# Gated mix of windowed decode attention and an MLP on one core: inputs transposed on VectorE, rest rows on 64 partitions, one exponential and one transpose per group, paired sums, a masked query product

## The chip, the core and the metric

The kernel runs on one core of a Trainium2 chip. A core has five engines, each with its own instruction stream: TensorE (PE in the profile, with its weight loads as PEld), VectorE (DVE), ScalarE (ACT), GpSimd (POOL) and SyncE (SP). SP and ACT issue loads from HBM; 16 DMA engines carry them out. Data is worked on in SBUF (128 partitions), and TensorE writes its products to PSUM (8 banks of 512 fp32 for each partition). Engines wait for each other and for loads by semaphores.

The metric is the device time of one execution in microseconds (us). The kernel before takes 368.27 us, the median of three runs (368.18 to 368.58).

## The reference

One decode step for 8 batch rows: attention over the last 2048 positions of a key and value cache (16 heads of keys and values, 32 query heads, so two query heads share one), and an MLP with a layer norm in front; a sigmoid gate mixes the two.

```python
B, D, Hq, Hkv, Sk, Dh, F = 8, 576, 32, 16, 8192, 128, 4608
W = 2048                                     # window: the last 2048 positions
g = sigmoid((x * gate_w).sum(-1, keepdims=True))
# a: attention
q = (x @ wq).reshape(B, 1, Hq, Dh)
k, v = k_cache[:, :, Sk - W:], v_cache[:, :, Sk - W:]   # each head of k, v serves two of q
p = softmax(einsum("bhqd,bhkd->bhqk", q, k) * Dh ** -0.5)
a = einsum("bhqk,bhkd->bhqd", p, v).reshape(B, 1, Hq * Dh) @ wo
# b: MLP
y = (x - mean(x)) / sqrt(var(x) + 1e-5)
b = gelu(y @ w1 + b1) @ w2 + b2
return g * a + (1 - g) * b                   # bf16 throughout; x is (8, 1, 576)
```

The inputs that matter for size are the two windows, 8 x 16 x 2048 x 128 bf16 each (67 MB each), wq and wo (4.7 MB each), w1 and w2 (5.3 MB each).

## The kernel before

**How it is planned.** The kernel is not written engine by engine. It adds operations, each with an engine, the operations it depends on and an estimated cost, to a plan (`_Plan`, L39). `schedule` (L62) runs a list schedule on those estimates and so fixes each engine's order; it then strikes out waits that others imply. `emit` (L176) writes the instructions of an engine in that order, with all waits of an operation ahead of its first instruction. On the chip each engine runs its list strictly in order; an operation whose input is late holds all that stands behind it.

**Slots.** Nine slots of 2 MB in SBUF (`NSLOT`, `take_slot` L679) take all big loads. SP issues the loads in the order of `stream` (L641 to L656): wq and w1 first (L450 to L454), then K units, from the sixth on in turn with V units, a block of wo after every eighth V unit, b2 and at last four pieces of w2 (the last one cut in four). A unit is half of one head's cache: four batch rows of that head, 128 partitions of 16 KB. A load waits until its slot has been read: K by the transposes on DVE (L748), V by the products with P (L795).

**Start.** ACT issues x, the gate vector (two loads) and b1 (L444 to L447). PE transposes x (`tr_in`, L482), b1 (`b1_fn`, L495) and the normalised y; DVE copies them from PSUM (L504, L509). DVE computes the gate's dot product, mean and variance on 8 partitions (L462 to L480). wq has 576 rows: 512 lie as four rows on each of 128 partitions, and the rest of 64 rows is cut in halves of columns, 128 half rows (L450); the stationary operand is padded with zeros in two forms (`xz`, L458) to fit. w1 is laid out the same way (L454). The query (`q_fn`, L541) and the MLP's first layer (`h`, L575) are made by four concurrent 32-column tiles of PE. The query is selected and spread to `q4` (L562 to L571). Slots 0 to 2 hold wq and slots 3 to 5 hold w1 until these products are done.

**A group** is two heads of K, four units (32 query rows: two heads, eight batch rows, two query heads each). For each half unit DVE transposes K in 32x32 blocks (L748) into one of two buffers, and PE multiplies with a block-diagonal query, two weight loads and eight matmuls of 512 columns (L754 to L761, helpers L395 and L410); the group's first product starts with a mask (L757). POOL fills the block-diagonal query with four copies (L737 to L742). After the fourth unit come, on DVE, the maximum over 2048 columns (L689) and ten small operations that combine it across partitions; on ACT four exponentials of 512 columns with their sums (L703); on DVE four transposes of P (L708) and the sums (L711, L712). `sums` (L715) adds across partitions on PE, takes reciprocals and scales by the gate (L724), once for each of the eight groups.

**V** (`v_batch`, L784): 64 matmuls on four tiles for each group of four units, a selection by three predicated copies (L811, L812), a fold on PE (L820), a copy on ACT (L826) and a scaling on POOL for each of two heads (L835). In the last group each unit is a batch of its own (`FULL`, L674). After every second group, eight query heads feed a product with a block of wo (L839 to L859).

**End.** All products with wo and w2, and b2, add up in one PSUM bank that `acc0` (L616) has cleared; DVE and ACT copy it out in halves (L891), and ACT stores it (L899).

## Time and profile before

| | |
|---|---|
| median of three runs | 368.27 us |
| the profiled execution | 368.25 us |
| its span, first to last instruction | 366.5 us |
| TensorE clock granted, mean | 0.81 |
| read from HBM | 154.31 MB |
| instructions | 2945 |

The span is the time from the first to the last instruction in the profile; the 1.75 us between span and time of the execution lie before and after. In the page's slices each digit is the busy share of a fortieth of the span (9.16 us) in tenths. Windows list, for each stretch, the busy time and count of PE, PEld, DVE, ACT and POOL, then PE's granted clock, the mean busy share of the 16 DMA engines and the GB/s that they moved. A row of the timeline has start, length, engine, line, operation, output and input, count and, in brackets, the idle time before it with what ended it. `DMA` rows in the chain of waits run from issue to landing; SPq and ACTq are rows in which SP or ACT issue a load. q1 is the queue of SP's loads, q10 of ACT's, q8 and q14 those of instructions.

### The profile page before, as it was taken

The numbers are of one execution on the slowest core, as the hardware profiler recorded it, in microseconds if no ns is written. First come the engines' busy times: TensorE is split into PE (matmuls) and PEld (weight loads), VectorE is DVE, ScalarE is ACT, GpSimd is POOL, SyncE is SP. The second block draws the span as 40 slices with busy tenths as digits, with TensorE's granted clock in tenths as the row PEclk, the third lists the DMA queues.
The fourth block names the chain that finished last, engine by engine and source line by source line (L and its number), as shares of the span: only waits on it lengthen the run. The fifth ranks groups of instructions, "written<-read, shape, count | busy, mean of one in ns | idle before, by whom it ended". The sixth has DMA issues, their size and how long they took to land.

```text
span 366.5 us, 2945 instructions
## 1 busy us (share of the span) xinstructions
PE 228.7 (62%) x1397; PEld 46.3 (13%) x935; DVE 227.1 (62%) x307; ACT 29.3 (8%) x84; POOL 25.6 (7%) x72
## 2 busy tenths in 40 slices
PE   0256972891974388762973298654975297666576
PEld 0211000100110012100210012000200022013233
DVE  0824999788585666549854665469654874566210
ACT  1010003003000110003000200003000300002000
POOL 8010001001010101001010101010000101001000
PEclk9986897997798869666996879686986679698558
DMA  8999999999999999999999999999999999999994
GB/s 342 429 405 427 429 435 434 433 436 429 427 429 431 428 432 435 431 431 428 429 430 428 424 439 431 429 433 431 427 431 429 435 430 431 431 429 425 424 429 196
DMA packets 11463, 154.52 MB, mean 422 GB/s; under 512 B 1300, under 2 KB 1588, under 8 KB 2104
## 3 DMA queue, kind: packets, MB, share of 16 engines
q1 hardware_dynamic: 11392, 154.29, 98.6%
q8 instruction: 9, 0.15, 0.1%
q10 hardware_dynamic: 56, 0.04, 0.1%
q14 instruction: 6, 0.05, 0.0%
HBM read 154.31 MB, written 0.01 MB: 421 GB/s over the span
## 4 chain that ended last, share of the span: by engine, by line
DMA 48%; DVE 23%; PE 20%; issue 3%; ACT 3%; SPq 2%
DMA arena<-in_A_k_cache_dram 33%; DVE arena L748 13%; PE ps L395 12%; DMA arena<-in_A_v_cache_dram 9%; DMA arena<-in_B_w_dram 6%; PE ps L410 5%; DVE arena L689 4%; PE ps L795 4%; ACT arena L703 3%; DVE arena L708 2%; DVE arena L698 1%; DVE arena L692 1%; SPq L776 1%; SPq L878 0%; SPq L453 0%
## 5 line engine op out<-in xcount | busy, mean ns | idle before, releaser
L748 DVE STREAM_TRANSPOSE arena<-arena 128x2048 f32<-128x2048 f32 x64 | 145.0, 2294 | 53.8 <-DMA arena<-in_A_k_cache_dram 48.2
L395 PE MATMUL ps<-arena 128*128 128x512 bf16 x402 | 138.4, 456 | 5.9 <-DVE arena L748 3.3
L410 PE MATMUL ps<-arena 128*128 128x512 bf16 x124 | 58.7, 473 | 80.9 <-ACT arena L703 40.7
L795 PE MATMUL ps<-arena 128*32 128x512 bf16 x512 | 36.9, 437 | 13.9 <-DMA arena<-in_A_v_cache_dram 13.9
L410 PEld LDWEIGHTS ps<-arena 128*128 128x128 bf16 x136 | 15.2, 112 | 210.6 <-DVE arena L748 90.0
L703 ACT ACTIVATE arena<-ps,arena 128x512 bf16<-128x512 f32 x32 | 21.5, 685 | 174.1 <-DVE arena L698 174.1
L689 DVE TENSOR_REDUCE arena<-ps 128x1 f32<-128x2048 f32 x8 | 18.3, 2287 | 21.8 <-PE ps L395 21.8
L708 DVE STREAM_TRANSPOSE arena<-arena 128x512 bf16<-128x512 bf16 x32 | 19.9, 675 | 0.8 <-ACT arena L703 0.8
L741 POOL COPY arena<-arena 32x128 bf16<-32x128 bf16 x32 | 9.2, 286 | 159.3 <-PE ps L395 148.0
L795 PEld LDWEIGHTS ps<-arena 128*32 128x32 bf16 x512 | 13.4, 106 | 46.9 <-issue 22.4
L835 POOL TENSOR_TENSOR arena<-arena 128x128 bf16<-128x128 f32 x16 | 7.8, 504 | 161.2 <-ACT arena L826 161.2
L718 DVE RECIPROCAL arena<-ps 128x32 f32<-128x32 f32 x8 | 2.9, 357 | 19.0 <-PE ps L717 19.0
L634 PE MATMUL ps<-arena 128*8 128x288 bf16 (+1 forms) x140 | 12.7, 337 | 1.5 <-DMA arena<-in_B_w_dram 1.1
L811 DVE COPY arena<-ps 128x128 f32<-128x128 f32 x11 | 3.0, 277 | 12.4 <-PE ps L795 12.4
L812 DVE COPY_PREDICATED arena<-arena,ps 128x128 f32<-128x128 int32 x33 | 9.9, 300 | 1.1
L826 ACT ACTIVATE arena<-ps 128x32 f32<-128x32 f32 (+1 forms) x9 | 1.7, 194 | 104.6 <-PE ps L820 104.6
L487 PE MATMUL ps<-arena 8*128 8x8 bf16 x8 | 0.6, 174 | 13.9 <-DVE arena L460 9.9
L820 PE MATMUL ps<-arena 128*128 128x32 f32 (+1 forms) x22 | 4.5, 283 | 6.6 <-DVE arena L812 6.6
L896 DVE CAST arena<-ps 8x288 bf16<-8x288 f32 x1 | 0.4, 445 | 12.4 <-PE ps L634 12.4
L401 PE MATMUL ps<-arena 128*32 128x512 bf16 (+1 forms) x48 | 6.0, 502 | 2.4 <-DMA arena<-in_B_w_dram 2.4
L634 PEld LDWEIGHTS ps<-arena 128*8 128x8 bf16 (+1 forms) x140 | 6.5, 98 | 6.4 <-DMA arena<-in_B_w_dram 2.6
L403 PE MATMUL ps<-arena 128*32 128x288 bf16 (+1 forms) x72 | 7.0, 473 | 0.0
(91 smaller groups left out, 74.7 us busy)
## 6 DMA issues: line engine op xcount, KB each, us to landing
arena<-in_A_k_cache_dram SPq DMA_DIRECT2D x32, 2048.0 KB, 28.5
arena<-in_A_v_cache_dram SPq DMA_DIRECT2D x32, 2048.0 KB, 28.5
arena<-in_B_w_dram SPq DMA_DIRECT2D x1, 4608.0 KB, 24.3
arena<-in_A_wo_dram SPq DMA_DIRECT2D x4, 1152.0 KB, 28.9
arena<-in_A_wq_dram SPq DMA_DIRECT2D x1, 4096.0 KB, 14.0
arena<-in_B_w_dram SPq DMA_DIRECT2D x3, 1296.0 KB, 20.0
arena<-in_B_w_dram SPq DMA_DIRECT2D x2, 576.0 KB, 22.5
arena<-in_A_wq_dram SPq DMA_DIRECT2D x1, 512.0 KB, 3.6
```

The lines of the kernel that those rows point to most:

```text
L395: return e.add_instruction(mybir.InstMatmult(name=nc.get_next_instruction_name(), ins=[e.lower_ap(rhs), e.lower_ap(lhsT)], outs=[e.lower_a ...
L403: mm = e.add_instruction(mybir.InstMatmult(name=nc.get_next_instruction_name(), ins=[e.lower_ap(r), e.lower_ap(lhsT)], outs=[e.lower_ap(o) ...
L410: mm = e.matmul(outs[0], lhsT, rhss[0], start=start, stop=stop)
L634: ins = e.matmul(ps[32 * j:32 * j + 8, BK_ACC, 0:JN], lhsT, rhs[:, JN * j:JN * j + JN], start=False, stop=True, skip_group_check=True, til ...
L689: mx = add("dve", lambda e: e.tensor_reduce(out=k(MX), in_=ps[:, 0:4, :].rearrange("p a n -> p (a n)"), axis=AXL.X, op=ALU.max), deps=[qk_ ...
L703: return e.activation(out=Pm[:, 512 * c:512 * c + 512], in_=ps[:, c, :], func=ACTF.Exp, bias=k(NB), scale=SCALE, accum_out=k(SUM + c))
L708: pts.append(add("dve", (lambda c=c: lambda e: e.transpose(bass.AP(arena, offset=aoffs("PT") + (g % 2) * 2048 + 128 * c, ap=[[AST, 128], [ ...
L741: return e.tensor_copy(dst, src)
L748: tr = add("dve", (lambda h=h, kb=kb: lambda e: e.transpose(bass.AP(arena_f, offset=foffs("KT") + kb * 2048, ap=[[AST // 2, 128], [1, 2048]]),
L795: mm = e.matmul(ps[32 * t:32 * t + 32, bank, :], PT[:, g % 2, q, 32 * r4:32 * r4 + 32], slot(s)[:, 512 * r4:512 * r4 + 512], start=(4 * c ...
L812: return e.copy_predicated(buf, bass.AP(arena_i, offset=foffs("m4") + r, ap=[[AST // 2, 128], [0, 128]]), src)
L835: return e.tensor_tensor(out=out_, in0=in0, in1=in1, op=ALU.mult)
```

## The change

Several edits come together.

- x is loaded four times and b1 in four parts, to partitions 0, 32, 64 and 96, over zeros that a POOL memset (`pad`) has written; DVE transposes x, y and b1 in 32x32 blocks. The PE transposes, their copies and the zero-padded pieces go. Statistics run on 128 partitions; the gate is spread by three copies and one DVE transpose.
- The rest rows of wq and w1 are 64 rows on 64 partitions; the fifth step of both products contracts over 64.
- The MLP's first layer writes three banks of 384 columns, in steps of 9 elements of the weights, so that one DVE transpose takes the place of four.
- One exponential of 2048 columns with one sum, and one transpose of P for each group; the maximum over four partitions' groups is one reduction.
- `sums` runs for two groups at once (four times), at another place of the stream.
- The block-diagonal query is one product with a mask on POOL; the mask matmuls of a group start before that query is ready (`late` waits, placed inside an operation). The wo rows' first matmul runs ahead of the wait for the block.
- In the last group the first two V units are one batch. `acc0` goes; the first product clears the bank. One POOL scaling for two heads.
- The pass that made POOL wait between narrow and wide operations goes.

```diff
@@ emit
+            parts = [[d for d in op.deps if d in part] for part in op.late]
+            for d in op.deps:
+                if not any(d in part for part in parts):
+                    wait(d, op)
+            self.parts = [lambda part=part, op=op: [wait(d, op) for d in part] for part in parts]
             inst = op.fn(handle)
@@ inputs
+        def late_wait():
+            P.parts.pop(0)()
+        o_pad = add("pool", lambda e: e.memset(view("pad").bitcast(F32), 0.0), name="pad", cost=1.6)
...
-        d_x = dma("act", lambda e: e.dma_start(x_sb, x2), "x", 8 * D * 2, name="d_x")
+        for q in range(4):
+            d_x.append(dma("act", (lambda q=q: lambda e: e.dma_start(x_sb[32 * q:32 * q + 8, :], x2))(), "x", 8 * D * 2, deps=[o_pad], name="d_x%d" % q, after=d_x[-1:]))
...
-        d_b1 = dma("act", lambda e: e.dma_start(b1c, B_b1.rearrange("(c f) -> c f", c=FC)), "b", F * 2, name="d_b1", after=[d_gw])
+        for q in range(4):
+            db.append(dma("act", (lambda q=q: lambda e: e.dma_start(b1c[32 * q:32 * q + FC, :], B_b1.rearrange("(c f) -> c f", c=FC)[:, 32 * FJ * q:32 * FJ * (q + 1)]))(), "b", F, deps=[o_pad], name="d_b1%d" % q, after=[d_gw1] + db[-1:]))
...
-        d_wqr = dma("sp", lambda e: e.dma_start(wq_r, A_wq[512:576, :].rearrange("k (s c) -> (k s) c", s=2)), "wq", 64 * 8192, name="d_wqr")
+        d_wqr = dma("sp", lambda e: e.dma_start(wq_r, A_wq[512:576, :]), "wq", 64 * 8192, name="d_wqr")
...
-        d_w1r = dma("sp", lambda e: e.dma_start(w1_r, B_w1[512:576, :].rearrange("k (s c) -> (k s) c", s=2)), "w1", 64 * F * 2, name="d_w1r", after=[d_w1m])
+        d_w1r = dma("sp", lambda e: e.dma_start(w1_r, B_w1[512:576, :]), "w1", 64 * F * 2, name="d_w1r", after=[d_w1m])
...
+        def spread(dst, name, deps, prio=0, s1=None):
+            ops = []
+            for n, (out_, in_) in enumerate([(dst[:, 0:4, :].rearrange("p t i -> p i t"), x_sb[:, 0:512].rearrange("p (i t) -> p i t", t=4))] +
+                                            [(dst[:, 4, 0:64], x_sb[:, 512:576])]):
+                if s1 is None:
+                    fn = (lambda out_=out_, in_=in_: lambda e: e.tensor_copy(out_, in_))()
+                else:
+                    fn = (lambda out_=out_, in_=in_: lambda e: e.tensor_scalar(out=out_, in0=in_, scalar1=s1[0], scalar2=s1[1], op0=ALU.add, op1=ALU.mult))()
+                ops.append(add("dve", fn, deps=deps, name="%ss%d" % (name, n), cost=0.4 if n == 0 else 0.15, prio=prio))
+            return ops, [add("dve", (lambda q=q: lambda e: e.transpose(view("%sT" % name)[32 * q:32 * q + 32, :].rearrange("p (t c) -> p t c", t=5), dst[32 * q:32 * q + 32, :, 32 * q:32 * q + 32]))(),
+                             deps=ops, name="%sT%d" % (name, q), cost=0.25, prio=prio) for q in range(4)]
+        o_xs, o_xT = spread(xb, "x", dx, prio=9)
+        o_b1T = add("dve", lambda e: e.transpose(b1T.rearrange("p (j c) -> p j c", c=32), b1c.rearrange("p (i j) -> p j i", j=FJ)), deps=db, name="b1T", cost=0.4)
@@ h (first layer of the MLP), for each t and qd
+                    kp = 128 if t < 4 else 64
+                    outs = [ps[32 * qd:32 * qd + 32, BK_H + k, 0:384] for k in range(3)]
+                    rhss = [bass.AP(arena, offset=aoffs("RAW") + W1O + F * t + 32 * FJ * qd + 3 * k, ap=[[AST, kp], [FCW, FC], [1, 3], [FJ, 32]]) for k in range(3)]
+                    ins = tile_row(e, qd, yT[0:kp, t, :], outs, rhss, t == 0, t == 4)
@@ softmax
-                    return e.activation(out=Pm[:, 512 * c:512 * c + 512], in_=ps[:, c, :], func=ACTF.Exp, bias=k(NB), scale=SCALE, accum_out=k(SUM + c))
+            ex = add("act", lambda e: e.activation(out=Pm, in_=ps[:, 0:4, :].rearrange("p a n -> p (a n)"), func=ACTF.Exp, bias=k(NB), scale=SCALE, accum_out=k(S)),
+                     deps=nbs + ([pt_done[g - 1]] if g else [o_hT]), name="exp%d" % g, cost=2.2, prio=5)
+            pt_done[g] = add("dve", lambda e: e.transpose(bass.AP(arena, offset=aoffs("PT") + (g % 2) * 2048, ap=[[AST, 128], [8, 64], [512, 4], [1, 8]]), Pm),
+                             deps=[ex] + ([pv_last[g - 2]] if g >= 2 else [o_u]), name="pt%d" % g, cost=2.4, prio=5)
@@ k_unit
-            for a in range(4 if q == 0 else 0):
+                    in0 = bass.AP(arena, offset=aoffs("q4") + 128 * g, ap=[[AST, 128], [8, 16], [0, 4], [1, 8]])
+                    in1 = bass.AP(arena_f, offset=foffs("mq"), ap=[[AST // 2, 128], [0, 16], [1, 4], [0, 8]])
+                    return e.tensor_tensor(out=dst, in0=in0, in1=in1, op=ALU.mult)
...
+                        mm_row(e, maskL, [ps[:, rc, :] for rc in range(2)], [maskR] * 2, True, False)
+                        late_wait()
+                        for rc in range(2, 4):
+                            held_mm(e, ps[:, rc, :], maskL, maskR, True, False)
+                        late_wait()
@@ stream and V
-                if vi % 4 == 0 and vi < NUQ:
+                if vi % 8 == 3:
                     stream.append(("S", vi // 4))
-        stream.insert(5, ("S", 0))
...
-            s = take_slot(UT, (3 - q) * 2 * UT + 10.0 if full else 4.0)
+            s = take_slot(UT, (3 - q if full else q == 0) * 2 * UT + (10.0 if full else 5.0))
...
-            if not full or q == 3:
+            if q == 3 or not full and q >= 1:
                 v_batch(g, list(v_wait))
```

More of the change, by code (lines that the diff above doesn't have):

```diff
@@ L116, in schedule @@
         self.makespan = max(op.t1 for op in self.all)
-        prev = None
-        for op in self.order["pool"]:
-            narrow = op.name.startswith("qr")
-            if prev is not None and narrow != prev.name.startswith("qr"):
-                op.deps.append(prev)
-            prev = op
         cnts = {}
@@ L466, in build_kernel @@
[L466 to L467 removed]
+        o_tq = [add("dve", (lambda q=q: lambda e: e.tensor_copy(cols[32 * q:32 * q + 32, C_T:C_T + 1], cols[0:32, C_T:C_T + 1]))(), deps=[o_t], name="tq%d" % q, cost=0.12) for q in range(1, 4)]
@@ L626, in __init__ @@
             def __init__(self, name, mms, deps, cost, after=(), prio=0):
+                first = not acc_groups
                 grp = self
```

391 lines of the change are left out of this document (170 added, 221 removed).

## The prediction

> **What bounds the kernel now.** I read the page's slices and DMA queues first, then the end of the run in windows of one microsecond, then the chain of waits, and last the timeline of the first 40 us.
>
> ```profile
> span 366.5 us, 2945 instructions
> PE 228.7 (62%) x1397; PEld 46.3 (13%) x935; DVE 227.1 (62%) x307; ACT 29.3 (8%) x84; POOL 25.6 (7%) x72
> ...
> DMA  8999999999999999999999999999999999999994
> GB/s 342 429 405 427 429 435 434 433 436 429 427 429 431 428 432 435 431 431 428 429 430 428 424 439 431 429 433 431 427 431 429 435 430 431 431 429 425 424 429 196
> ...
> q1 hardware_dynamic: 11392, 154.29, 98.6%
> q8 instruction: 9, 0.15, 0.1%
> q10 hardware_dynamic: 56, 0.04, 0.1%
> q14 instruction: 6, 0.05, 0.0%
> ```
>
> The loads on q1 (the queue that SP fills) occupy the 16 DMA engines for 98.6% of the span; no compute engine is above 62%. The rate is about 430 GB/s (26.9 per engine) in nearly every slice, although these slices move different tensors in rows of different length. So the kernel ends when 154.29 MB have gone through, and an edit counts if it changes the bytes, the rate, the start or the end of this stream, or lets its queue run empty.
>
> ```profile
> 360.00:361.00 1.00, 0.35 (x8) 0.18 (x6) 0.00 (x0) 0.00 (x0) 0.00 (x0) 1.00 0.93 370
> 361.00:362.00 1.00, 1.00 (x18) 0.54 (x12) 0.00 (x0) 0.00 (x0) 0.00 (x0) 1.00 0.71 262
> 362.00:363.00 1.00, 0.71 (x10) 0.27 (x8) 0.00 (x0) 0.00 (x0) 0.00 (x0) 1.00 0.18 69
> 363.00:364.00 1.00, 0.71 (x10) 0.31 (x10) 0.00 (x0) 0.00 (x0) 0.00 (x0) 1.00 0.07 24
> ```
> ```profile
> 343.01 20.90 DMA arena<-in_B_w_dram
> 363.96 0.31 PE ps L634 x2
> 364.29 0.45 DVE arena L896
> ```
>
> The column before the last is the DMA share. After 362 it is 0.18 and 0.07: about three engines of 16, then one, still work while the others are done (0.18 x 16 = 2.9). The last w2 piece lands at 363.91 (343.01 + 20.90), and its two matmuls, the copy-out and the store follow. The end is set by the latest DMA engine, some 1.5 us behind most of the others.
>
> **The change, part by part.** The sum is made against the profiled execution, 368.25 us (span 366.5 and 1.75 around it); the median of the runs is 368.27, so they agree.
>
> *Rest rows on 64 partitions.* The last 64 rows of wq and w1 were cut in two, 128 half rows; now they are 64 whole rows. Bytes stay the same.
>
> ```profile
> arena<-in_A_wq_dram SPq DMA_DIRECT2D x1, 512.0 KB, 3.6
> arena<-in_B_w_dram SPq DMA_DIRECT2D x2, 576.0 KB, 22.5
> ```
>
> (One of the two 576 KB loads is w1's.) At 430 GB/s they take 0.52/0.430 = 1.22 and 0.59/0.430 = 1.37 us. No load of the trace goes to 64 partitions, so I bound it. Below: nothing, if each engine keeps its 26.9 GB/s whatever the destination. Above: half the rate, if half of the partitions take in half as much: +1.22 + 1.37 = +2.6 us, paid by all engines, in a stream that has no gap to hide it. The slices' rate is the same for every source and row length; what all these loads share is 16 engines and 128 destination partitions, and the edit changes the second. I take 2.4, near the upper end: engines that come to the second load at different moments, as they come to the end above, find the other's share free for a while. [...]
>
> *Shorter programs.* q8 and q14 load instructions through the same 16 engines. 0.15 MB over PE's 2332 instructions (1397 + 935) is 64 B each, and nine loads are one per 256 instructions. The new program has 49 matmuls and 43 weight loads fewer (the small transposes, acc0, four of eight softmax sums), with fp32 ones counted twice some 2250 in all: below 2304, so eight loads. DVE, ACT and POOL shrink by some 45, 40 and 35 instructions: about two of q14's six loads go. Each 16 KB load holds one engine for 16.4 KB / 26.9 = 0.6 us, where the matrix loads are dealt out evenly; this is what can make three engines late. Bounds: nothing, if the loads that go sat on engines with time to spare; -1.5 us, if they made all the late ones late. Three of 15 go, so I take -0.6.
>
> *Inputs transposed on DVE.* ACT now issues 10 small loads instead of four, after a POOL memset, and b1's transpose is the seventh instruction on DVE.
>
> ```profile
> 3.96 1.79 POOL L441 MEMSET arena<- 128x2048 bf16 x1
> ...
> 0.79 0.57 ACTq L444 DMA_DIRECT2D arena<-in_A_x_dram  x1
> 1.40 0.59 ACTq L445 DMA_DIRECT2D arena<-in_gate_w_dram  x2
> 2.02 0.28 ACTq L447 DMA_DIRECT2D arena<-in_B_b_dram  x1
> ...
> 9.57 0.29 DVE L460 COPY arena<-arena 8x64 bf16<-8x64 bf16 x2 [9.57 <-DMA arena<-in_gate_w_dram]
> 18.53 0.29 DVE L538 TENSOR_TENSOR arena<-arena 128x128 f32<-128x128 f32 x1
> 22.60 1.31 DVE L559 STREAM_TRANSPOSE arena<-arena 128x512 bf16<-128x512 bf16 x2
> 32.35 4.50 DVE L748 STREAM_TRANSPOSE arena<-arena 128x2048 f32<-128x2048 f32 x2 [8.45 <-DMA arena<-in_A_k_cache_dram]
> ```
> ```profile
> 12.19 0.69 PE L499 MATMUL ps<-arena 4*128 4x4 bf16 x9 [1.92 <-DMA arena<-in_B_b_dram]
> 27.50 0.45 PE L401 MATMUL ps<-arena 128*32 128x288 bf16 x4 [2.40 <-DMA arena<-in_B_w_dram]
> 31.86 0.30 PE L403 MATMUL ps<-arena 128*32 128x288 bf16 x4
> 34.95 1.36 PE L395 MATMUL ps<-arena 128*128 128x512 bf16 x3 [2.79 <-DVE arena L748]
> ```
>
> Loads that were issued by 2.3 us were used at 9.57 (the third) and 12.19 (the fourth): between the big rows a small load advances by one per 2.6 us. The memset of 1360 words is some 1.2 us by L441's 1.79 for 2048. So six loads (x four times, gate twice) land at 9.57 + 3 x 2.6 + 1.2 = 18.6 at most, and b1's four at up to 29; I take 28, the first ones being quicker. q_pe needs xT alone: about 2 us later than now, hidden, since three K units are queued. But b1T stands ahead of gate, layer norm, yT, qT and every K transpose on DVE. What DVE did from 9.57 to 18.82 (9.3 us, with little idle) and from 21.9 to 23.91 (2 us) now begins at 28 and ends near 39: K's first transpose starts 7 us late. PE is held too: the selection of q waits for DVE, and h_pe stands behind it. h_pe took 4.7 us (27.50 to 32.16) for 80 matmuls of 288 columns; now it is 60 of 384, the same columns in steps of 18 bytes. Bounds: 4.7, and 60 x 0.45 x 384/288 = 36 us if no two of its tiles overlap any more; I take 6, near the row. K's first product then starts at 39 + 1.4 + 6 = 46 instead of 34.95: 11 us late. What hides this is the queue of loads. It is thinnest here:
>
> ```profile
> 94.40 20.71 DMA arena<-in_A_k_cache_dram
> 115.14 2.32 DVE arena L748
> ```
> ```profile
> 102.09 0.54 SPq L776 DMA_DIRECT2D arena<-in_A_v_cache_dram  x1
> ```
> ```profile
> 90.72 3.60 PE L795 MATMUL ps<-arena 128*32 128x512 bf16 x32 [7.51 <-DMA arena<-in_A_v_cache_dram]
> ```
>
> SP issues K11 at 94.40, and it lands 20.71 later; a unit moves in 2.10/0.430 = 4.9 us, so V6, issued at 102.09, lands near 120.0. Off its 17.9 go 4.9 and about 2 for issue and landing: 11 us to spare, 13 with the stream itself 2.4 later; and PE's wait of 7.51 for V before 90.72 takes up part of a delay. So 11 us late costs nothing, by a margin of 2 to 5 us.
>
> *The rest* is off the path. One exponential of 2048 replaces four, and one transpose four:
>
> ```profile
> L748 DVE STREAM_TRANSPOSE arena<-arena 128x2048 f32<-128x2048 f32 x64 | 145.0, 2294 | 53.8 <-DMA arena<-in_A_k_cache_dram 48.2
> L703 ACT ACTIVATE arena<-ps,arena 128x512 bf16<-128x512 f32 x32 | 21.5, 685 | 174.1 <-DVE arena L698 174.1
> L708 DVE STREAM_TRANSPOSE arena<-arena 128x512 bf16<-128x512 bf16 x32 | 19.9, 675 | 0.8 <-ACT arena L703 0.8
> L741 POOL COPY arena<-arena 32x128 bf16<-32x128 bf16 x32 | 9.2, 286 | 159.3 <-PE ps L395 148.0
> ```
>
> Between 0.7 and 2.7 us for the exponential (4 x 685), 2.3 to 2.7 for the transpose by L748 and L708; the transpose no longer runs beside the exponential, so P^T is ready some 1 to 2 us later, and PV waits for V anyway. The masked product is one POOL instruction for four L741, 0.3 to 1.1 us, and PE's mask matmuls run before that wait. The paired sums come a group later; their readers, the output scalings, feed wo blocks due much later. In the last group V's first two units share a batch, so one slot is freed 4.9 us later; the last w2 pieces were issued 20.9 us ahead. SP's order of loads is unchanged. Cover gone, each of these costs its own microsecond or two per group. I enter 0.
>
> Sum: 368.25 + 2.4 - 0.6 = 370.0 us.
>
> **The rivals.** *B: not slower.* The rest rows cost nothing, because an engine's own 26.9 GB/s is the limit, and the shorter programs free the late engines: 368.25 - 1.1 = 367.1. For it: 430 is 16 times the same number in every slice. Against: nothing in the trace separates engine from destination.
> *C: the queue runs empty.* Near K11 and V6, when the start is more than 13 to 16 us late; each microsecond more costs one. For it: h_pe's new stride and b1's place on DVE. Against: the margin. If h_pe takes 12 us, and what it delays has the narrower margin, the start is 17 us late: 370.0 + 4 = 374. [...]
> *D: nothing to see.* The loads cost about 1.0 and the late engines give 0.9 back: 368.4.
>
> **How the numbers follow.** Forecast 0.55, B 0.18, C 0.17, D 0.10. A measurement here can tell 0.2% (0.74 us) from no change. Forecast and C are slower: 0.72; D is the same: 0.10; B is faster: 0.18. The likeliest's own range is 369.0 to 371.4 (loads 1.5 to 2.6, end 0 to -1.0, 0.5 for what I put at nothing). The range 366.8 to 373.8 takes in most of B and half of C, and leaves out less than 0.2.
>
> **What would show it.** The rest rows: the window just after the first bytes at half of 430 GB/s for some 2.4 us, and another near 25 us. Shorter programs: q8 with eight loads, q14 with about four, and a share at the end that falls more steeply. The start: DVE's b1 transpose at 26 to 29, K's first transpose near 39, h_pe's length. The queue: no slice after the second under 400 GB/s; a dip near 110 us is C. I am wrong if the rate never dips and the time falls.

## The result and the profile after

The changed kernel takes 374.94 us (median of six runs, 374.44 to 375.35), the kernel before 368.38 us beside it (six runs, 368.18 to 368.61). The ratio is 1.0176 with a 95% interval of 1.0163 to 1.0189: 6.5 us slower. The spans of the profiled executions are 372.8 and 366.5 us. It went as rival C has it (374), not as the forecast (370.0). Of all the executions below one, of rest64_alone (378.60 us), fell into a slower state and is left out of the figures.

The page of the changed kernel, its slices of 9.32 us and its queues:

```profile
span 372.8 us, 2704 instructions
...
DMA  7999999999996999999999999999999999999995
GB/s 282 419 378 407 433 425 435 431 424 436 434 403 255 424 434 425 434 433 424 438 431 424 436 424 441 425 425 438 431 424 436 425 440 425 434 431 427 425 429 238
...
q1 hardware_dynamic: 11264, 154.29, 97.8%
q8 instruction: 9, 0.15, 0.1%
q10 hardware_dynamic: 128, 0.06, 0.1%
q14 instruction: 3, 0.02, 0.0%
```

The bytes are the same, and the rate is again 430 GB/s nearly everywhere. Two things are new. The first slice moves 282 GB/s where it moved 342, and the third 378 where it moved 405. And the thirteenth, 111.8 to 121.2 us, moves 255: the queue was empty for part of it. Two windows of three microseconds there, with the DMA share and the GB/s in the last two columns:

```profile
111.00:114.00 3.00, 2.40 (x48) 0.96 (x36) 2.96 (x3) 0.00 (x0) 0.00 (x0) 1.00 0.11 44
114.00:117.00 3.00, 2.46 (x23) 0.53 (x18) 3.00 (x3) 0.00 (x0) 0.00 (x0) 1.00 0.48 175
```

Against 430 GB/s, (386 + 255) x 3 / 430 = 4.5 us are missing. SP's timeline and its waits between 90 and 120 us say why:

```profile
114.27 0.53 SPq L697 DMA_DIRECT2D arena<-in_A_k_cache_dram  x1
117.30 0.53 SPq L751 DMA_DIRECT2D arena<-in_A_v_cache_dram  x1
```
```profile
SPq L697 <- DVE arena L713: 19.9, 2, 16.1
```

K11 and V6 are the units that the prediction named (K and V units counted from 0). K11 goes out at 114.27, where it went out at 94.40, and V6 at 117.30 (102.09). SP waits 16.1 us for DVE to have transposed the unit whose slot K11 takes. This is the queue running empty at the place that rival C named. The start that it comes from, on DVE and then on PE:

```profile
21.14 1.32 DVE L470 COPY arena<-arena 128x512 bf16<-128x512 bf16 x2 [21.14 <-DMA arena<-in_gate_w_dram]
29.42 0.69 DVE L478 STREAM_TRANSPOSE arena<-arena 128x288 bf16<-128x288 bf16 x1 [5.55 <-DMA arena<-in_B_b_dram]
42.92 4.46 DVE L713 STREAM_TRANSPOSE arena<-arena 128x2048 f32<-128x2048 f32 x2
```
```profile
43.06 1.15 PE L548 MATMUL ps<-arena 128*128 128x256 bf16 x4 [14.54 <-DVE arena L542]
44.13 0.92 PE L408 MATMUL ps<-arena 128*32 128x384 bf16 x4
44.84 1.61 PE L410 MATMUL ps<-arena 128*32 128x384 bf16 x8
...
53.32 1.59 PE L410 MATMUL ps<-arena 64*32 64x384 bf16 x8
55.07 0.81 PE L402 MATMUL ps<-arena 128*128 128x512 bf16 x3 [0.16 <-issue]
```

DVE starts when the sixth small load lands (21.14), stands 5.55 us for b1's four, and reaches K at 42.92 (32.35 before). PE waits 14.5 us for q's transposes, then does the first layer from 44.13 to 54.91, 10.8 us, and K's first products start at 55.07: 20.1 us late, against 34.95 before. The forecast had 11.

The slower first and third slice are the rest rows, the last 64 rows of wq and of w1. Windows with their rate in the last column, the kernel before first, then the changed one:

```profile
2.00:4.00 2.00, 0.00 (x0) 0.00 (x0) 0.00 (x0) 1.28 (x1) 2.00 (x11) 1.00 1.23 476
4.00:6.00 2.00, 0.00 (x0) 0.00 (x0) 0.00 (x0) 0.00 (x0) 2.00 (x3) 1.00 0.86 348
24.00:26.00 2.00, 1.10 (x4) 0.27 (x4) 0.00 (x0) 0.86 (x1) 0.00 (x0) 0.71 0.87 355
26.00:28.00 2.00, 0.50 (x12) 0.12 (x4) 0.00 (x0) 0.16 (x1) 1.14 (x4) 0.50 1.02 434
28.00:30.00 2.00, 2.00 (x40) 0.34 (x8) 0.00 (x0) 0.00 (x0) 0.00 (x0) 0.50 0.97 418
```
```profile
2.00:4.00 2.00, 0.00 (x0) 0.00 (x0) 0.00 (x0) 0.00 (x0) 1.96 (x10) 1.00 1.18 311
4.00:6.00 2.00, 0.00 (x0) 0.00 (x0) 0.00 (x0) 0.00 (x0) 2.00 (x3) 1.00 0.93 311
24.00:26.00 2.00, 1.98 (x20) 0.51 (x12) 0.00 (x0) 0.00 (x0) 0.00 (x0) 1.00 1.01 384
26.00:28.00 2.00, 2.00 (x24) 0.30 (x8) 0.00 (x0) 0.00 (x0) 0.00 (x0) 1.00 0.96 195
28.00:30.00 2.00, 0.51 (x8) 0.00 (x0) 0.58 (x1) 0.00 (x0) 0.00 (x0) 1.00 1.05 333
```

The five rates sum to 2031 and to 1534: (2031 - 1534) x 2 / 430 = 2.3 us less moved. Note that the DMA share is 0.96 in the window of 195 GB/s and 1.02 in that of 434: the engines count as busy in both, so the share does not show this loss and the GB/s do.

So 2.3 and 4.5 us account for 6.8, a little more than the 6.3 between the spans. The experiments take these terms apart one by one.

### The profile page after: what moved, and what is told of

It reads as the page before. It is cut to its first block, busy times and chain, and to the rows that moved or that the text cites. A ratio compares the mean times of both kernels' runs of the same rounds, so it can differ in the third digit from the quotient of the medians.

```text
span 372.8 us, 2704 instructions
## 1 busy us (share of the span) xinstructions
PE 220.8 (59%) x1342; PEld 41.7 (11%) x892; DVE 225.0 (60%) x249; ACT 23.8 (6%) x36; POOL 23.3 (6%) x38
## 3 DMA queue, kind: packets, MB, share of 16 engines
q1 hardware_dynamic: 11264, 154.29, 97.8%
## 4 chain that ended last, share of the span: by engine, by line
DMA 43%; DVE 28%; PE 21%; ACT 3%; issue 2%; ACTq 1%; SPq 1%; POOL 1%; POOLq 0%
DMA arena<-in_A_k_cache_dram 22%; DVE arena L713 16%; PE ps L402 11%; DMA arena<-in_A_v_cache_dram 9%; DMA arena<-in_B_b_dram 6%; DMA arena<-in_B_w_dram 5%; PE ps L417 4%; DVE arena L663 4%; ACT arena L672 3%; PE ps L771 3%; PE ps L410 2%; PE ps L408 1%; DVE arena L670 1%; DVE arena L788 1%; SPq L860 1%
## 5 line engine op out<-in xcount | busy, mean ns | idle before, releaser
L402 PE MATMUL ps<-arena 128*128 128x512 bf16 x404 | 133.4, 442 | 11.5 <-DVE arena L713 10.1
L417 PE MATMUL ps<-arena 128*128 128x512 bf16 x122 | 55.9, 458 | 81.9 <-DVE arena L713 41.4
L771 PE MATMUL ps<-arena 128*32 128x512 bf16 x512 | 34.6, 417 | 4.3 <-DMA arena<-in_A_v_cache_dram 4.3
L672 ACT ACTIVATE arena<-ps,arena 128x2048 bf16<-128x2048 f32 x8 | 15.7, 1968 | 169.6 <-DVE arena L670 169.6
L408 PE MATMUL ps<-arena 128*32 128x512 bf16 (+3 forms) x40 | 7.8, 747 | 24.0 <-DVE arena L474 24.0
L675 DVE STREAM_TRANSPOSE arena<-arena 128x2048 bf16<-128x2048 bf16 x8 | 18.2, 2274 | 2.1 <-ACT arena L672 2.1
L706 POOL TENSOR_TENSOR arena<-arena 128x512 bf16<-128x512 bf16 x8 | 8.3, 1040 | 151.8 <-PE ps L402 142.1
L814 POOL TENSOR_TENSOR arena<-arena 128x256 bf16<-128x256 f32 (+1 forms) x9 | 6.0, 666 | 157.9 <-ACT arena L805 157.9
L410 PE MATMUL ps<-arena 128*32 128x384 bf16 (+3 forms) x60 | 11.3, 789 | 0.0
L548 PE MATMUL ps<-arena 128*128 128x256 bf16 x4 | 1.1, 408 | 14.5 <-DVE arena L542 14.5
L796 PE MATMUL ps<-arena 128*128 128x32 f32 (+2 forms) x20 | 4.1, 286 | 8.5 <-DVE arena L788 8.5
L685 DVE RECIPROCAL arena<-ps 128x64 f32<-128x64 f32 x4 | 2.2, 560 | 7.6 <-PE ps L684 7.6
```

The costliest lines, as they stand in the source:

```text
L402: return e.add_instruction(mybir.InstMatmult(name=nc.get_next_instruction_name(), ins=[e.lower_ap(rhs), e.lower_ap(lhsT)], outs=[e.lower_a ...
L408: mm = e.matmul(outs[0], lhsT, rhss[0], start=start, stop=stop, skip_group_check=True, tile_position=pos)
L410: mm = e.add_instruction(mybir.InstMatmult(name=nc.get_next_instruction_name(), ins=[e.lower_ap(r), e.lower_ap(lhsT)], outs=[e.lower_ap(o) ...
L417: mm = e.matmul(outs[0], lhsT, rhss[0], start=start, stop=stop)
L672: ex = add("act", lambda e: e.activation(out=Pm, in_=ps[:, 0:4, :].rearrange("p a n -> p (a n)"), func=ACTF.Exp, bias=k(NB), scale=SCALE, ...
L675: pt_done[g] = add("dve", lambda e: e.transpose(bass.AP(arena, offset=aoffs("PT") + (g % 2) * 2048, ap=[[AST, 128], [8, 64], [512, 4], [1, ...
```

## The experiments

In each group the same kernel before was run beside the others; ratios are to it.

**Are the rest rows a cost of their own, and what of them costs?** *rest64_alone* is the kernel before with these lines alone, and the two loads and the readers of the rows to match:

```diff
-        wq_r = RAW[:, 4 * 4096:4 * 4096 + 2048]
+        wq_r = RAW[0:64, 4 * 4096:5 * 4096]
...
-        w1_r = RAW[:, W1O + 4 * F:W1O + 4 * F + F // 2]
+        w1_r = RAW[0:64, W1O + 4 * F:W1O + 5 * F]
```

> The kernel before with one part of the change alone: the last 64 rows of wq and w1 go to 64 partitions. Theory (rest rows cost by themselves, the late start is a second, separate loss): +2.4 to +2.6 us on the kernel before, near 371.0, no dry slice of the queue near 111 us, and two windows at about half of 430 GB/s, just after the first bytes and near 26 us. Rival (rest rows cost nothing; all 6.6 us come from the start and the dry queue): within 0.5 us of the kernel before, 368.4.

Measured: 370.72 us against 368.12, ratio 1.0069 (1.0052 to 1.0085): +2.5 us, no dry slice, and windows near half rate:

```profile
2.00:4.00 2.00, 0.00 (x0) 0.00 (x0) 0.00 (x0) 1.28 (x1) 2.00 (x11) 1.00 0.96 258
4.00:6.00 2.00, 0.00 (x0) 0.00 (x0) 0.00 (x0) 0.00 (x0) 2.00 (x3) 1.00 0.88 270
24.00:26.00 2.00, 0.00 (x0) 0.00 (x0) 0.00 (x0) 0.74 (x1) 1.07 (x4) 0.50 1.12 419
26.00:28.00 2.00, 0.00 (x0) 0.00 (x0) 0.00 (x0) 0.00 (x0) 0.07 (x1) 0.50 0.96 203
28.00:30.00 2.00, 0.73 (x16) 0.16 (x8) 0.00 (x0) 0.00 (x0) 0.00 (x0) 0.50 0.96 360
```

The sum is 1510, (2031 - 1510) x 2 / 430 = 2.4 us less than before. Two more kernels ask what in it costs. *rest64_half_rows* cuts each row into two pieces that lie 128 bytes apart, so that the packets are as short and as many as in the kernel before (shown against rest64_alone; the rows of w1 likewise, not shown):

```diff
-        wq_r = RAW[0:64, 4 * 4096:5 * 4096]
+        wq_r = RAW[0:64, 4 * 4096:4 * 4096 + 2 * 2112].rearrange("p (s c) -> p s c", s=2)[:, :, 0:2048]
```

> The kernel of rest64_alone with each rest row in two pieces that lie 128 bytes apart on its partition: 128 packets of 4 and 4.5 KB, as in the kernel before, into 64 partitions, as in the change. Theory (64 destination partitions are what costs): +2.5 us as in rest64_alone, near 370.7, with the same two windows at half rate. Rival (64 long packets are dealt out badly over 16 engines; 128 short ones are not): within 0.5 us of the kernel before, 368.2.

Measured: 370.86 us, ratio 1.0068 (1.0052 to 1.0083), as with whole rows. The length and number of the packets are not what costs. *rest64_even* sends the 64 whole rows to other partitions. It loads them and waits for them, but its products leave them out, so it shows the price of the load and not a way to use the rows (shown against rest64_alone):

```diff
-        wq_r = RAW[0:64, 4 * 4096:5 * 4096]
+        wq_r = RAW[0:128:2, 4 * 4096:5 * 4096]
...
-        w1_r = RAW[0:64, W1O + 4 * F:W1O + 5 * F]
+        w1_r = RAW[0:128:2, W1O + 4 * F:W1O + 5 * F]
```

> The kernel of rest64_alone with the 64 whole rest rows on the 64 even partitions 0, 2, ... 126 in place of partitions 0 to 63. The rows are loaded and waited for, but not read: the fifth step of both products reads the fourth row group again, so the rest rows' part of the result is left out. If the number of destination partitions is what costs: +2.5 us on the kernel before, 370.7, windows at half rate. If it is which partitions (the lower half alone), because only half of the paths into the memory are used: within 0.6 us of 368.2, and no window under 350 GB/s at 26 to 28 us. I take the second for the likelier.

Measured: 368.40 us against 368.25, ratio 1.0006 (0.9997 to 1.0015), and at the place of the 203 GB/s:

```profile
2.00:4.00 2.00, 0.00 (x0) 0.00 (x0) 0.00 (x0) 1.28 (x1) 2.00 (x11) 1.00 1.37 528
4.00:6.00 2.00, 0.00 (x0) 0.00 (x0) 0.00 (x0) 0.00 (x0) 2.00 (x3) 1.00 0.63 263
24.00:26.00 2.00, 0.00 (x0) 0.00 (x0) 0.00 (x0) 0.00 (x0) 0.80 (x3) 0.50 0.93 385
26.00:28.00 2.00, 1.46 (x28) 0.31 (x8) 0.00 (x0) 0.00 (x0) 0.00 (x0) 0.50 1.02 434
28.00:30.00 2.00, 2.00 (x48) 0.41 (x12) 0.00 (x0) 0.00 (x0) 0.00 (x0) 0.69 0.94 401
```

The sum is 2011, close to the 2031 of the kernel before. Sixty-four partitions cost nothing that can be told when they are spread over all 128; on the lower 64 the rate falls to 203 GB/s.

**What empties the queue?** Two kernels each take one part out of the changed kernel's start. *h_contiguous_in_after* has the first layer's product as before, and the four transposes behind it (not shown):

```diff
-                    outs = [ps[32 * qd:32 * qd + 32, BK_H + k, 0:384] for k in range(3)]
-                    rhss = [bass.AP(arena, offset=aoffs("RAW") + W1O + F * t + 32 * FJ * qd + 3 * k, ap=[[AST, kp], [FCW, FC], [1, 3], [FJ, 32]]) for k in range(3)]
+                    outs = [ps[32 * qd:32 * qd + 32, BK_H + c, 0:32 * FJ] for c in range(FC)]
+                    rhss = [RAW[0:kp, W1O + F * t + FCW * c + 32 * FJ * qd:W1O + F * t + FCW * c + 32 * FJ * (qd + 1)] for c in range(FC)]
```

> The changed kernel with the first layer's product as before: four banks of 288 contiguous columns and four transposes behind it, in place of three banks of 384 columns in 18-byte steps. Theory (the late start empties the queue, and the strided product is 6 us of the lateness): h_pe takes 4.7 us in place of 10.8, K's first product starts near 49 in place of 54.9, K11 is issued 6 us sooner, the dry spell (4.7 us) shrinks to under 1 us, and the time falls by about 4 us, to 370.9. Rival (the dry spell comes from what was regrouped in the heads: one exponential, paired sums, other groups of V): h_pe shorter, but the dry spell stays at 4 to 5 us, and the time within 0.7 us of 374.9.

*b1T_later_in_after* moves the line of `o_b1T` behind that of `o_qT`, and the first layer no longer waits for it:

```diff
-        o_b1T = add("dve", lambda e: e.transpose(b1T.rearrange("p (j c) -> p j c", c=32), b1c.rearrange("p (i j) -> p j i", j=FJ)), deps=db, name="b1T", cost=0.4)
...
+        o_b1T = add("dve", lambda e: e.transpose(b1T.rearrange("p (j c) -> p j c", c=32), b1c.rearrange("p (i j) -> p j i", j=FJ)), deps=db, after=o_qT, name="b1T", cost=0.4)
...
-            o_hch.append(add("pe", fn, deps=dw1 + o_yT + [o_gb, o_b1T] + o_qe, name="h_pe%d" % t, cost=1.9, after=o_hch[-1:]))
+            o_hch.append(add("pe", fn, deps=dw1 + o_yT + [o_gb] + o_qe, name="h_pe%d" % t, cost=1.9, after=o_hch[-1:]))
```

> The changed kernel with b1's transpose on VectorE placed behind those of q, so that gate, layer norm and y no longer stand behind b1's loads; h_pe no longer waits for it. Theory (late start): VectorE's first transpose of K starts near 37 in place of 42.9, K's first product near 49 in place of 54.9 with h_pe still at 10.8 us; the dry spell shrinks to under 1 us, and the time falls by about 4 us, to 370.9. Rival (regrouped heads): the start moves, the dry spell stays, within 0.7 us of 374.9. A third: only the strided product matters (PE is late in any case), K's first product moves by under 2 us, and the time by under 2 us.

Measured: 370.47 us, ratio 1.0061 (1.0046 to 1.0076), and 370.62 us, ratio 1.0064 (1.0047 to 1.0081). Each one alone takes the dry spell away. The slices of the first and of the second:

```profile
GB/s 285 423 373 396 434 427 426 427 437 430 437 430 419 428 435 428 427 430 430 439 428 432 424 438 427 428 428 428 439 430 430 425 439 428 428 430 427 426 430 232
```
```profile
GB/s 285 423 365 386 431 437 429 431 426 428 440 426 424 435 419 435 435 428 428 428 437 433 424 435 433 427 430 428 435 430 431 427 436 430 430 428 431 425 428 227
```

Where 255 stood, 419 and 424 stand. Both keep the regrouped heads, so these alone do not empty the queue. *single_loads_in_after* loads x and b1 once and copies them on DVE (the added lines):

```diff
+        d_x = [dma("act", lambda e: e.dma_start(x_sb[0:8, :], x2), "x", 8 * D * 2, deps=[o_pad], name="d_x0")]
...
+        d_b1 = dma("act", lambda e: e.dma_start(b1raw, B_b1.rearrange("(c f) -> c f", c=FC)), "b", F * 2, name="d_b1", after=[d_gw1])
...
+        o_x4 = [add("dve", (lambda q=q: lambda e: e.tensor_copy(x_sb[32 * q:32 * q + 8, :], x_sb[0:8, :]))(), deps=dx0, name="x4_%d" % q, cost=0.3, prio=9) for q in range(1, 4)]
...
+        db = [add("dve", (lambda q=q: lambda e: e.tensor_copy(b1c[32 * q:32 * q + FC, :], b1raw[:, 32 * FJ * q:32 * FJ * (q + 1)]))(), deps=[d_b1, o_pad], name="b14_%d" % q, cost=0.2) for q in range(4)]
```

> The changed kernel with x and b1 loaded once, as before the change (4 small loads in place of 10), and copied to the other quadrants of partitions by seven VectorE copies; strided first layer, rest rows and b1's place as in the change. Theory (the small loads advance by one per 2.5 us between the big rows, and that is the first half of the lateness): the first copy starts at 10 to 11 in place of 21.1, b1's transpose at 14 to 17 in place of 29.4, VectorE's first transpose of K at 32 to 34, h_pe as soon as w1 is there (29.5), K's first product near 41, no dry slice, and the time 370.0 to 370.6 (only the rest rows are left). Rival (the number of loads does not matter, the strided product alone is too late): over 372.

Measured: 369.83 us, ratio 1.0040 (1.0027 to 1.0054). The first copy started at 14.39 (10 to 11 was expected), b1's transpose at 19.77 (14 to 17), K's first products at 44.39 (41), with the strided product still in place; the time is 0.2 us under the 370.0 to 370.6 expected. So three different cures of the same lateness all take the dry spell away, and a fourth kernel has the strided product without any other lateness. *strided_h_alone* is the kernel before with it (its last step, and the one transpose behind it, are not shown):

```diff
-                    outs = [ps[32 * qd:32 * qd + 32, BK_H + c, 0:32 * FJ] for c in range(FC)]
...
+                        outs = [ps[32 * qd:32 * qd + 32, BK_H + k, 0:384] for k in range(3)]
+                        rhss = [bass.AP(arena, offset=aoffs("RAW") + W1O + F * t + 32 * FJ * qd + 3 * k, ap=[[AST, 128], [FCW, FC], [1, 3], [FJ, 32]]) for k in range(3)]
```

> The kernel before with the strided first layer alone (three banks of 384 columns in 18-byte steps, one transpose behind it). Theory: h_pe takes 10.8 us in place of 4.7, K's first product starts near 41 (6 us late), inside the 11 to 14 us that the queue has to spare at K11 and V6, so the time stays within 0.5 us of 368.1. Rival (the strided product costs by itself, wherever it stands): 4 us slower, 372.

Measured: 368.25 us against 368.17, ratio 1.0001 (0.9992 to 1.0010), though the product does take 10.7 us (26.89 to 37.59); each step of 12 matmuls is again 2.1 us long. It makes K's first products only 2.8 us late (37.75; 6 was expected), since they waited for K's first unit and its transpose until 34.95 in any case:

```profile
26.89 0.92 PE L401 MATMUL ps<-arena 128*32 128x384 bf16 x4 [1.52 <-DMA arena<-in_B_w_dram]
27.59 1.61 PE L403 MATMUL ps<-arena 128*32 128x384 bf16 x8
28.99 0.90 PE L401 MATMUL ps<-arena 128*32 128x384 bf16 x4
```

The last two runs of this kind have nothing of the change. *start_held_12* and *start_held_8* put twelve or eight idle transposes on DVE ahead of K's first, which waits for them:

```diff
+        for i in range(12):
+            tr_hist.append(add("dve", lambda e: e.transpose(bass.AP(arena_f, offset=foffs("KT") + 2048, ap=[[AST // 2, 128], [1, 2048]]),
+                                                            bass.AP(arena_f, offset=foffs("ones_bf"), ap=[[AST // 2, 128], [0, 8], [1, 256]])),
+                               deps=[o_ones] + tr_hist[-1:], name="hold%d" % i, cost=2.3, after=o_qT, prio=9))
```

> The kernel before with nothing of the change: eight transposes of a constant (2.3 us each, their result is overwritten) stand on VectorE ahead of the first transpose of K, so that the start is late by itself. K's first transpose at about 42.3 in place of 32.35, first product at 44.6, 9.7 us late. Theory (a late start is free as long as the queue has units, 11 to 14 us): within 0.5 us of 368.1. Rival (a late start costs its own time at once): +9.

> The same with twelve such transposes: K's first transpose at about 51.5, first product at 53.8, 18.9 us late (in the changed kernel it is 20). Theory: the spare time of K11 is 94.40 + 20.71 less 4.9 for its own transfer and about 2 for issue and landing, 13.9 us, so the queue is dry for about 5 us near 111 us and the time is 372 to 374, with none of the change's other parts in it. Rival (the dry spell of the changed kernel comes from its regrouped heads): within 1 us of 368.1.

Measured: 369.80 us, ratio 1.0042 (1.0028 to 1.0056), with K's products at 46.26, 11.3 us late (9.7 was expected); and 376.08 us, ratio 1.0219 (1.0200 to 1.0238), with them at 55.77, 20.8 us late. A late start by itself is thus enough for a loss like the changed kernel's. Eight lost 1.6 us, more than the 0.5 of the theory and far less than the 9 of the rival. My figure for twelve was too low (372 to 374), since a second dry stretch came up that I had not foreseen. Windows of start_held_12:

```profile
52.00:56.00 4.00, 0.64 (x2) 0.10 (x1) 4.00 (x7) 0.32 (x1) 0.00 (x0) 0.50 0.74 315
56.00:60.00 4.00, 4.00 (x14) 0.49 (x5) 2.42 (x3) 0.12 (x1) 0.00 (x0) 0.68 0.26 100
...
111.00:114.00 3.00, 2.66 (x7) 0.26 (x2) 2.93 (x7) 0.28 (x2) 0.00 (x0) 0.50 0.71 300
114.00:117.00 3.00, 2.84 (x9) 0.76 (x3) 1.09 (x1) 0.13 (x1) 0.00 (x0) 0.56 0.30 93
```

Between 52 and 60 us the queue runs out, since DVE has only just begun to free slots: SP's first load after the wait goes out at 57.89, and (115 + 330) x 4 / 430 = 4.1 us are missing. Then 3.3 us near 111. In the changed kernel DVE itself starts K at 42.92 and only PE is later; the same load goes out at 47.42, and the first of the two stretches does not come.

One number ties these kernels together. K11 goes out 58 to 61 us after K's first products, whatever the body is:

| kernel | K's first products, us | K11 issued, us | later by |
|---|---|---|---|
| before | 34.95 | 94.40 | 59.5 |
| strided_h_alone | 37.75 | 95.61 | 57.9 |
| single_loads_in_after | 44.39 | 103.95 | 59.6 |
| start_held_8 | 46.26 | 106.39 | 60.1 |
| h_contiguous_in_after | 48.90 | 109.33 | 60.4 |
| b1T_later_in_after | 49.41 | 109.86 | 60.5 |
| rest128_in_after | 52.47 | 112.93 | 60.5 |
| after | 55.07 | 114.27 | 59.2 |
| start_held_12 | 55.77 | 115.12 | 59.4 |

The loss begins where this time passes an edge. With the rest rows on 64 partitions, the windows from 108 to 114 us miss 0.3 us when K11 goes out at 109.33 (h_contiguous_in_after) and 0.1 at 109.86 (b1T_later_in_after), and the changed kernel misses 4.5 at 114.27. If each microsecond past the edge costs one, the edge lies near 109.8, and the first two agree with that. Without the rest rows the stream is 2.3 us earlier, and so the edge should be, near 107.5. By that estimate rest128_in_after misses 112.93 - 107.5 = 5.4 (5.3 in its windows, below), and start_held_12, whose stream the first dry stretch has already held up by 4.1, misses 115.12 - 107.5 - 4.1 = 3.5 (3.3). start_held_8 stands just before this edge, and it is not sharp: its traced execution (368.83 us) misses 0.7 in two windows of 377 GB/s, and its ten executions lie between 368.31 and 371.03.

**Do the terms add?** *rest128_in_after* is the changed kernel with the rest rows back on 128 partitions and two slots of xT and yT for their halves (the rows of wq; those of w1 and the readers are not shown):

```diff
-        wq_r = RAW[0:64, 4 * 4096:5 * 4096]
+        wq_r = RAW[:, 4 * 4096:4 * 4096 + 2048]
...
-        d_wqr = dma("sp", lambda e: e.dma_start(wq_r, A_wq[512:576, :]), "wq", 64 * 8192, name="d_wqr")
+        d_wqr = dma("sp", lambda e: e.dma_start(wq_r, A_wq[512:576, :].rearrange("k (s c) -> (k s) c", s=2)), "wq", 64 * 8192, name="d_wqr")
```

> The changed kernel with the rest rows back on 128 partitions as half rows. If the costs simply add, 2.5 us less than the changed kernel, 372.4. Theory of the late start: the loads in front of the queue pass 2.6 us sooner, but the slots come free at times set by the small loads, by VectorE and by the first layer, which move by about 1.3 us at most (only wq's rest rows are ahead of b1's loads), so that the dry spell near 111 us grows from 4.7 to about 6 and the time falls by 0.3 to 1.6 us only, to about 374.0.

Measured: 372.63 us (371.83 to 373.33), ratio 1.0120 (1.0104 to 1.0136), 0.56% or 2.1 us under the changed kernel's ratio: between the 2.5 of plain addition and the 0.3 to 1.6 expected. The profiled execution, the slowest of its four, has a span of 371.6, 1.2 us less than that of the changed kernel, and its windows show the reason that was given:

```profile
108.00:111.00 3.00, 3.00 (x37) 1.49 (x38) 1.57 (x3) 0.00 (x0) 0.00 (x0) 0.74 0.40 169
111.00:114.00 3.00, 2.20 (x29) 0.51 (x18) 3.00 (x2) 0.00 (x0) 0.00 (x0) 1.00 0.02 5
114.00:117.00 3.00, 3.00 (x27) 0.53 (x18) 3.00 (x2) 0.00 (x0) 0.00 (x0) 1.00 0.92 350
```

(261 + 425 + 80) x 3 / 430 = 5.3 us are missing, 0.8 more than with the rows on 64. The queue is drained sooner and stays dry longer. How much of the 2.5 that gives back, the runs leave open. Where the queue has time to spare, the two terms do add: *fixes_rest64* has the edits of h_contiguous_in_after and b1T_later_in_after together, *three_fixes_in_after* that of rest128_in_after too.

> The changed kernel with the contiguous first layer and b1's later transpose, rest rows on 64 partitions as in the change. Theory (three terms that add once the queue has time to spare): 367.5 + 2.5 = 370.0, no dry slice, K's first product near 43. If one of the two fixes alone had left a part of the dry spell (K11 was issued at 109.3 and 109.9 with one fix each), this is up to 0.6 us under the 370.5 and 370.6 of those; if not, the same 370.5.

> The changed kernel with three parts undone together: rest rows on 128 partitions, the contiguous first layer, b1's transpose behind those of q. What stays of the change: fewer instructions (DVE-transposed inputs, one exponential and one transpose per group, paired sums, masked query product). Theory (rest rows and the empty queue are the whole loss; the shorter programs free late engines): K's first product near 43, no dry slice, the first K unit lands at 31 to 32 as before the change, and the time is 0 to 1.5 us under the kernel before, 367.5 if the prediction's 0.6 holds. Rival (something else in the regrouped heads costs): 369 or more.

Measured: 370.33 us, ratio 1.0055 (1.0041 to 1.0069), as with either fix alone, and 367.50 us against 368.17, ratio 0.9981 (0.9973 to 0.9990). From these the change is made up: -0.7 us for what three_fixes_in_after keeps of it, +2.7 for the rest rows (1.0055 - 0.9981 = 0.74%), +4.5 for the empty queue (1.0176 - 1.0055 = 1.21%), together the 6.5. That they add up to the whole follows from how they are taken; what checks them is that the second is near the 2.5 of rest64_alone, and the third is the 4.5 that is missing from the windows.

**Where do the 0.7 us come from?** *fixes_padded_programs* and *fixes_long_programs* add 6 and 64 tiny copies per group on ACT and on POOL to three_fixes_in_after (the second is shown):

```diff
+            for j in range(64):
+                padA.append(add("act", lambda e, j=j: e.activation(out=scr[:, j:j + 1], in_=k(S), func=ACTF.Copy), deps=[ex] + (padA[-1:] if j == 0 else []), after=padA[-1:], name="padA%d_%d" % (g, j), cost=0.2, prio=-1))
+                padP.append(add("pool", lambda e, j=j: e.tensor_copy(scr[:, 64 + j:65 + j], k(S)), deps=[ex] + (padP[-1:] if j == 0 else []), after=padP[-1:], name="padP%d_%d" % (g, j), cost=0.2, prio=-1))
```

> The kernel of three_fixes_in_after with 6 tiny ScalarE and 6 tiny GpSimd copies added per group (one column each, read by nothing), so that the programs of these two engines are as long as before the change (84 instructions on ScalarE, 86 on GpSimd against 84 and 72). Theory (the 0.7 us that three_fixes_in_after gained is instruction loads that no longer hold single DMA engines back): q14 loads rise from 3 to 5 or 6, one or two engines end 1.5 us behind the median again, and the time goes back to 368.0 to 368.3. Rival (the gain has another source): within 0.2 us of 367.5.

> The kernel of three_fixes_in_after with 64 tiny ScalarE and 64 tiny GpSimd copies added per group (one column each, read by nothing), 512 more on each engine: about eight more instruction loads (q14 at 9 to 12). Theory (each load holds one DMA engine back for good, some 0.2 us of end each, as the prediction had it): 368.8 to 369.3. Rival (loads land on engines with time to spare, the 0.7 us come from elsewhere): within 0.4 us of 367.5.

Measured: 367.75 us, ratio 0.9982 (0.9973 to 0.9991), with five loads on q14, between the two expectations by its median and as three_fixes_in_after by its ratio; and 368.51 us, ratio 1.0009 (1.0000 to 1.0017), with eleven. The second instruction queue of the second kernel, and the end of three_fixes_in_after and then of it (DMA share and GB/s last):

```profile
q14 instruction: 11, 0.09, 0.1%
```
```profile
362.00:363.00 1.00, 0.69 (x10) 0.29 (x10) 0.00 (x0) 0.00 (x0) 0.00 (x0) 1.00 0.12 38
363.00:364.00 1.00, 0.27 (x2) 0.06 (x2) 0.45 (x1) 0.40 (x1) 0.00 (x0) 1.00 0.00 0
```
```profile
362.00:363.00 1.00, 0.89 (x12) 0.27 (x8) 0.00 (x0) 0.00 (x0) 0.00 (x0) 1.00 0.32 112
363.00:364.00 1.00, 0.59 (x8) 0.27 (x8) 0.00 (x0) 0.00 (x0) 0.00 (x0) 1.00 0.08 27
```

Eight more loads (3 to 11) come with 0.28%, 1.0 us, and late engines are back at the end. That is some 0.13 us for each load if the 1024 copies themselves cost nothing, which no run separates. Neither of my two figures for it (368.8 at least, 367.9 at most) held: the price is between. Two more loads would be 0.25 us, which fixes_padded_programs cannot tell from nothing. *fixes_single_loads* adds the single loads of x and b1 to three_fixes_in_after:

> The kernel of three_fixes_in_after with x and b1 loaded once and copied on VectorE (4 small loads in place of 10). The start has time to spare in both, so the theory gives 367.5, the same within 0.3 us; if the six extra small loads hold single engines back as instruction loads may, 367.0 to 367.2.

Measured: 366.99 us (366.87 to 367.07) against 368.25, ratio 0.9966 (0.9953 to 0.9978), with K's first products at 37.63. It is the fastest of all, 1.25 us under the kernel before. Its runs all lie under those of three_fixes_in_after (367.25 to 367.98), though the intervals of the two ratios overlap; six small loads fewer are worth some 0.15%, 0.55 us, with no dry spell in either.

## Why the prediction was wrong, point by point

**The bound, right.** One stream of 154.29 MB at 430 GB/s sets the time; every gain and loss above is a change of its rate, its gaps or its end.

**Rest rows, right in size.** Forecast +2.4 between 0 and 2.6, measured 2.5 alone and 2.7 between fixes_rest64 and three_fixes_in_after. The reason given, half of the partitions, was only half of it: it is which 64 of them. With the rows on partitions 0 to 63 the window from 26 to 28 us moved 195 GB/s in the changed kernel, 203 in rest64_alone and 235 in rest64_half_rows; with the rows on the even partitions (rest64_even) it moved 434, as in the kernel before. The runs show rates and partitions, not the way that a load takes into the memory: the half of the paths in the expectation of rest64_even is the author's conjecture.

**Shorter programs, right in size, in part by luck.** -0.6 was forecast and -0.7 (0.4 to 1.0) found, although q8 stayed at nine loads (eight were forecast, and PE has 2234 instructions in the changed kernel, fewer than the 2250 of the forecast; one load per 256 instructions was the author's estimate, and here it gave one too few) and q14 fell to three (four). At 0.13 us a load, three fewer are 0.4, and the change's six extra small loads, which the forecast put at nothing here, take 0.55 the other way. If these add, some 0.8 of the gain lies elsewhere in what three_fixes_in_after keeps; no run shows where.

**The start, the step that failed.** "So 11 us late costs nothing, by a margin of 2 to 5 us": the margin was right and the lateness was not. The edge at 109.8 for K11 is 15.4 us behind the 94.40 of the kernel before, inside the 13 to 16 of the prediction; but the start was 20.1 us late, and 4.5 us were lost where 0 was entered. The largest part is h_pe, the first layer's product: "I take 6, near the row" of bounds 4.7 to 36, where 10.8 was measured, 4.8 us too little. The other is DVE's chain, taken to end near 39 and ending at 42.92: b1 landed at 29.42 in place of 28, and the chain behind it takes 13.5 us in place of 11. On that chain are now b1's own transpose (0.69), y's copies at 1.44 (0.51 and 0.30 before) and four transposes of y (1.38); that its operations run on 128 partitions costs nothing (0.73 us for 576 columns, on 8 partitions and on 128). Together 3.9 + 4.8 = 8.7 of the 9.1 us.

**Rival C, right in mechanism, place and causes.** It named K11 and V6, h_pe's stride and b1's place, "if h_pe takes 12 us", and 374. h_contiguous_in_after and b1T_later_in_after show that it takes both causes: either alone, with the rest of the change, leaves no dry spell. Its number came out of other parts than it gave, 17 us late with 4 lost, where 20.1 late lost 4.5. What was wrong is the chance of 0.17, which followed from taking a price near the lower bound of h_pe. The rows now show that price: in steps of 18 bytes the 4608 columns of a step (12 matmuls of 384) took 2.09 us in the changed kernel, contiguous (16 matmuls of 288) 0.96 in the kernel before, both at a granted clock of 0.50.

**The rest, right.** The regrouped heads cost nothing on balance: with them three_fixes_in_after is faster than the kernel before, and the interval from K's first products to K11 is the same within 3 us. Rivals B and D fall with rest64_alone.

## What to carry to other kernels

Where a stream has slack in one place, add up the lateness of every step ahead of it, each at the unfavourable end of its bounds: two delays that were free alone were 4.5 us together, and undoing either was enough. A price between 4.7 and 36 us that sits next to a margin of 2 to 5 us has to be measured before anything is concluded from "near the row". Look at GB/s beside the DMA share: rows for the lower 64 partitions kept the engines busy (share 0.96) at 195 GB/s.

## What the runs showed of the hardware that was not expected

- 64 rows on the even partitions load at the full rate, 434 GB/s in the window where the same rows on partitions 0 to 63 move at 203.
- A matmul's moving operand in steps of 18 bytes cost the same at two clocks: 2.09 us per 12 matmuls of 384 columns, at a granted clock of 0.50 (44 to 48 us of the changed kernel) and of 1.00 (27 to 35 us of strided_h_alone). The lower clock did not make it worse:

```profile
44.00:46.00 2.00, 2.00 (x13) 0.28 (x8) 2.00 (x2) 1.02 (x1) 0.66 (x1) 0.50 1.01 434
```
```profile
27.00:29.00 2.00, 2.00 (x13) 0.17 (x6) 0.00 (x0) 0.00 (x0) 0.69 (x3) 1.00 0.94 401
```

- The same three small loads on ACT's queue, x and the gate vector's two, were first used at 6.55 us in rest64_half_rows, 8.09 in rest64_alone, 9.57 in the kernel before and 14.39 in single_loads_in_after, although they were issued by 3.3 us in each. A small load between large rows has no landing time here that could be counted on.
- Small loads and instruction loads were not free beside a full stream: some 0.09 us for each small load (six for 0.55 us), and 0.13 us for each instruction load (eight for 1.0 us) if the copies that brought them cost nothing.
